# Soft-MoE behind banded attention: the last projection rounds dealt differently between output steps, one step split in two, three weight loads split in two

## The chip, the cores and the metric

One core of one Trainium2 chip runs the whole program. The metric is the time of one execution on the device in microseconds, and the median of three runs counts. Engines are named as in the profile: PE (TensorE, matmuls), DVE (VectorE), ACT (ScalarE), POOL (GpSimd) and SP (SyncE, which only issues transfers). SPq or PEq means the sequencer of an engine.

## The reference

Attention over 4 batches, 8 heads, 768 tokens and 64 features of a head, with a band of 96 keys, 8 global keys and a distance bias, is followed by a soft mixture of experts. Its tail is what this case is about:

```python
slot_input = d.T @ x                       # 32 slots, 4 for each of 8 experts
for e in range(E):
    h = np.maximum(slot_input[e] @ w1[e], 0.0)      # [4, 1024]
    slot_out[e] = h @ w2[e]                          # [4, 512]
c = softmax(logits, over the slots)        # [3072 tokens, 32 slots]
return c @ slot_out                        # [3072, 512], 6.29 MB in float32
```

## The kernel before

The first 140 us are attention and the softmax statistics, written as a long list of steps in a fixed order (`ORDER`); nothing there is touched. The tail follows in straight code at the end of `tile_attention_moe`, and the order in which it is written is the order on each engine: a manual schedule, in which every engine runs its instructions one after the other.

**Weights.** The two weight matrices of the experts lie in 32 pieces of 128 x 2048 float32 (1 MB). 24 of them have places of their own; the last eight (numbers 24 to 31, the second half of `w2` of experts 0 to 7) are loaded into places that the hidden layer has read. `load_w` issues them on SP, each as a first half (columns 0 to 1023) and a second half (1024 to 2047). Those second halves are the last loads of the program. The SP queue allows eight transfers under way: each issue waits for the landing of the one eight places before it.

**Projection.** The 512 output features are made in three parts, `OUT_PART`: 256, 128 and 128 wide. For a part, `project` multiplies the hidden values of all experts by `w2` in 16 rounds (eight blocks of the hidden dimension, for experts 0 to 3 and then 4 to 7); a round is four matmuls, one for each expert, each done in two passes in float32, and all rounds of a part add into one PSUM bank (line 154). `project_rounds(n, first, past)` issues some of the 16. Part 2 reads the second halves of pieces 24 to 31: rounds 0 to 7 those of pieces 24 to 27, rounds 8 to 15 those of 28 to 31.

**Slots.** When a part's rounds are done, `slots_raw` copies the bank to SBUF (ACT, line 183), `slots_spread` multiplies it by a spreading matrix (PE, line 192) and copies the result to the tile `sos` (DVE or ACT, line 193).

**Combine.** `combine(n, step)` makes output: four PSUM banks, one for each batch, and for each of the step's token tiles one matmul per batch (line 206); then ACT and DVE copy two banks each into halves of a staging buffer (line 211), and SP issues one transfer for batches 0 and 1 and one for 2 and 3 (line 212). `STEPS` says which token tiles a step has. The banks come from a ring of six (`LeftBanks`), so a step reuses banks of earlier steps and waits until those are copied. The staging halves are used in turn: `tb`, `v`, `tt`, `ph`, `xtt`, `xta`, `ph`, and again from `tb`.

**Order.** Rounds of part 1 stand between the steps of part 0, and rounds of part 2 around the steps of part 1, so that PE has work while a step's copies and transfers run. The steps of part 2 come last, one behind the other.

**The end.** Each engine then reads a flag and branches over a general path, which these inputs do not need (line 989). Behind it SP waits for its eight transfer semaphores, in the order of their numbers, and the engines meet at a barrier (line 1189).

Of the kernel before, what the change touches and what calls it, by code (L numbers as in the profile page):

```python
# [42 lines left out]
NS = E * SPE  # L43
HF = DM // 2
OUT_PART = ((0, 256), (256, 128), (384, 128))
STEPS = (tuple((0, 256, t, k) for t, k in ((0, 1), (1, 1), (2, 2), (4, 2))), tuple((0, 128, t, 3) for t in (0, 3)), tuple((0, 128, t, 2) for t in (0, 2, 4)))
BLOCKS = [(n, *step) for n in range(len(OUT_PART)) for step in STEPS[n]]
BLOCK_AT = [sum(4 * w * k for _, _, w, _, k in BLOCKS[:i]) for i in range(len(BLOCKS) + 1)]
XH = NJ * HF
# [19 lines left out]
class Moe:  # L69
# [125 lines left out]
    def combine(self, ps, ct, n, so, obs, out, step):  # L195


        nc = self.nc
        f, w, t0, k = STEPS[n][step]
        at = BLOCK_AT[sum(map(len, STEPS[:n])) + step]  # L200
        cps = [ps.tile([P, 512], F32, name="cp", tag="x") for _ in range(B)]
# [97 lines left out]
def tile_attention_moe(ctx: ExitStack, tc: tile.TileContext, qk, v, phi, w1, w2, nn, out):  # L299
# [29 lines left out]
    WP = 2048  # L329
# [46 lines left out]
    npl = len(places)  # L376
# [11 lines left out]
    def piece(k):  # L388
        m, r = divmod(k, 16)
        if m == 0:  # L390
            a, r = divmod(r, 8)
            half, s = divmod(r, 4)
        else:
            half, r = divmod(r, 8)
            a, s = divmod(r, 4)
        return m, 4 * a + s, half
# [3 lines left out]
    def load_w(pieces, c0=0, c1=WP):  # L400

        for k in pieces:
            m, e, half = piece(k)
            nc.sync.dma_start(out=places[k][:, c0:c1], in_=(w1, w2)[m][e][:, WP * half + c0:WP * half + c1])
# [520 lines left out]

    moe.hidden(left, Moe.slot_view(sl), w1_of, hs, ht, (reuse_first, reuse_second))
    load_w([31], WP // 4, WP // 2)
    load_w(range(npl + 1, 32), WP // 2, WP)

    obs = [places[16 + i // 2][:, 1024 * (i % 2):1024 * (i % 2) + 1024] for i in range(2 * (npl - 16))]  # L930
    ops = [xx[:, 0]]
# [2 lines left out]
    def project(n, a, cs=range(8)):  # L934
        moe.project(ops[n], ht, lambda e, h: places[where[1, e, h]], n, a, cs)
# [4 lines left out]
    def slots_raw(n):  # L940
        moe.slots_raw(ops[n], ows[:, parts[n]])

    def slots_spread(n, *copies):
        moe.slots_spread(left, ows[:, parts[n]], sos[:, parts[n]], copies)

    def combine(n, *steps):
        for step in steps:
            moe.combine(left, ct, n, sos[:, parts[n]], obs, out, step)

    def project_rounds(n, first, past):  # L950
        for k in range(first, past):
            project(n, k // 8, (k % 8,))
# [10 lines left out]
    weights(range(4), nc.vector.tensor_copy)  # L963
    slots_spread(0, nc.scalar.copy, nc.scalar.copy)
    ops += [left.keep(ops[0])] * 2
    project_rounds(1, 0, 4)
    combine(0, 0)
    project_rounds(1, 4, 7)
    combine(0, 1)
    project_rounds(1, 7, 11)  # L970
    combine(0, 2)
    project_rounds(1, 11, 16)
    slots_raw(1)
    combine(0, 3)
    slots_spread(1, nc.vector.tensor_copy)
    project_rounds(2, 0, 4)
    combine(1, 0)
    project_rounds(2, 4, 16)
    slots_raw(2)
    combine(1, 1)  # L980
    slots_spread(2, nc.vector.tensor_copy)
    combine(2, 0, 1, 2)
    order.close()
# [9 lines left out]
def general(ctx, tc, moe, qk, v, phis, w1, w2, ngl, nlo, ident, out):  # L993
# [114 lines left out]
    with ExitStack() as g3:  # L1108
# [27 lines left out]
        for n, (at, w) in enumerate(OUT_PART):  # L1136
# [5 lines left out]
            moe.slots_spread(ps, ow[:, c], so[:, c], (nc.vector.tensor_copy, nc.scalar.copy))  # L1142
            for step in range(len(STEPS[n])):
                moe.combine(ps, ct, n, so[:, c], obs, out, step)
# [53 lines left out]
```

## Time and profile before

| | us |
|---|---|
| median of 3 runs (187.65 to 188.02) | 187.96 |
| the profiled execution | 187.57 |
| its span in the profile | 185.6 |
| PE busy, share of the span | 169.5, 91% |
| DVE busy | 143.0, 77% |
| ACT busy | 125.5, 68% |
| POOL busy | 91.6, 49% |

The span is what the engines' instructions cover; the rest of the execution's 187.57 us lies around it. The shares are means over stages with different limits: PE is busy in nine slices of ten almost to the end, POOL has almost nothing to do from 125 us on, and in the last slices DMA is busy at 0.7 to 0.9 of its 16 engines while ACT and DVE are mostly idle. What a change in the tail does is read from the tail.

### The profile page before, as it was taken

What the parts mean: (1) busy time and instruction counts of PE and PEld (TensorE: products, weight loads), DVE (VectorE), ACT (ScalarE), POOL (GpSimd) and SP (SyncE); (2) the same over time, 40 slices, a digit from 0 to 9 for tenths busy, and PEclk for the clock granted to TensorE, in tenths of its full rate; (3) what the DMA queues carried; (4) which work ended last, traced back from release to release, by engine and by line L of the source; (5) the groups of instructions that cost most, each with busy time, mean ns of one, the idle gap of its engine ahead of it and who ended that gap; (6) DMA issues with size and microseconds to landing.
All of it is one profiled execution on the core that took longest, in us unless ns stands there. A gap on an engine that the chain in (4) does not pass through costs nothing. (4 is left out here: it accounts for less than half of the span.)

```text
span 185.6 us, 6743 instructions
## 1 busy us (share of the span) xinstructions
PE 169.5 (91%) x2811; PEld 126.4 (68%) x2811; DVE 143.0 (77%) x382; ACT 125.5 (68%) x163; POOL 91.6 (49%) x121
## 2 busy tenths in 40 slices
PE   8899899999998999999999997989899999999720
PEld 2567689897887698888879896674443256678610
DVE  5999999999999999899999899984686203345430
ACT  3499989999987989999999999933302110344320
POOL 6826689769868679588788778620010000000000
PEclk9999999999999999999999999999999999999995
DMA  6999999998998966979966699999999999889791
GB/s 204 415 414 369 405 403 385 360 368 248 379 342 319 361 203 169 390 272 333 371 221 201 222 289 412 401 346 408 353 354 331 419 401 411 350 308 400 300 351 45
DMA packets 15306, 61.41 MB, mean 331 GB/s; under 512 B 1698, under 2 KB 2850, under 8 KB 13474
## 3 DMA queue, kind: packets, MB, share of 16 engines
q1 hardware_dynamic: 15264, 60.89, 87.9%
q8 instruction: 24, 0.39, 0.8%
q14 instruction: 16, 0.13, 0.2%
q10 hardware_dynamic: 2, 0.00, 0.0%
HBM read 54.59 MB, written 6.29 MB: 328 GB/s over the span
## 5 line engine op out<-in xcount | busy, mean ns | idle before, releaser
L592 POOL TENSOR_TENSOR ph<-tb,ph 128x432 f16<-128x432 f32 x78 | 82.3, 1084 | 28.4 <-ACT ph L585 26.6
L582 ACT ACTIVATE tb<-tb,nb 128x1296 f32<-128x1296 f32 x32 | 43.5, 1374 | 1.6 <-DVE nb L578 1.5
L609 PEld LDWEIGHTS <-ph 128*128 128x128 f16 x1248 | 41.4, 97 | 3.8 <-issue 3.2
L609 PE MATMUL x<-v,ph 128*128 128x65 f16 (+1 forms) x1248 | 43.1, 193 | 0.4
L585 ACT CAST ph<-tb 128x1296 f16<-128x1296 f32 x32 | 40.7, 1271 | 3.1 <-PE x L609 1.9
L557 PE MATMUL sc<-raw 64*128 64x216 f32 (+1 forms) x392 | 39.3, 338 | 1.3 <-DVE mx L566 1.3
L557 PEld LDWEIGHTS sc<-raw 64*128 64x128 f32 x392 | 32.3, 186 | 6.1 <-DVE mx L566 2.7
L634 DVE CUSTOM_DVE_ANT_1 xn<-x,rc 120x448 f32<-120x448 f32 x32 | 18.8, 621 | 0.6
L566 DVE CUSTOM_DVE_ANT_1 tb<-sc,tt,mx 128x864 f32<-128x864 f32 x16 | 17.8, 1114 | 1.0 <-POOL ph L592 0.4
L646 PE MATMUL m<-ident,xn 120*128 120x120 f32 x105 | 16.1, 277 | 2.1 <-DVE nb L578 1.0
L535 DVE SCALAR_TENSOR_TENSOR v<-vt,v 128x896 f16<-128x896 f32 x14 | 15.2, 1085 | 0.2
L646 PEld LDWEIGHTS m<-ident,xn 120*128 120x128 f32 x105 | 10.7, 140 | 5.6 <-DVE nb L578 1.4
L592 DVE TENSOR_TENSOR ph<-tb,ph 128x432 f16<-128x432 f32 x18 | 13.4, 761 | 0.0
L101 PE MATMUL hp<-wp,sl 128*32 128x512 f32 x80 | 10.7, 593 | 0.0
L206 PE MATMUL cp<-sos,ct 32*128 32x128 f32 (+1 forms) x116 | 8.2, 332 | 1.3 <-DVE sos L193 1.1
L566 DVE CUSTOM_DVE_ANT_1 tb<-sc,xtt,mx 128x864 f32<-128x864 f32 x8 | 8.9, 1112 | 0.5 <-PE sc L557 0.4
L566 DVE CUSTOM_DVE_ANT_1 tb<-sc,xta,mx 128x864 f32<-128x864 f32 x8 | 8.8, 1101 | 0.1
L528 ACT ACTIVATE v<-vt 128x896 f16<-128x896 f32 x9 | 8.6, 953 | 0.0
L566 DVE CUSTOM_DVE_ANT_1 tb<-sc,tt 128x864 f32<-128x864 f32 x8 | 8.4, 1052 | 0.0
L154 PE MATMUL o<-wp,ht 128*32 128x128 f32 x256 | 8.2, 275 | 0.0
L154 PEld LDWEIGHTS o<-wp,ht 128*32 128x32 f32 x256 | 6.6, 110 | 1.4 <-issue 1.0
L101 PEld LDWEIGHTS hp<-wp,sl 128*32 128x32 f32 x80 | 2.9, 110 | 6.6 <-issue 6.3
(220 smaller groups left out, 277.7 us busy)
## 6 DMA issues: line engine op xcount, KB each, us to landing
raw<-in_qk_dram SPq DMA_DIRECT2D x14, 832.0 KB, 5.9
wp<-in_w_dram SPq DMA_DIRECT2D x10, 1024.0 KB, 8.1
wp<-in_w_dram SPq DMA_DIRECT2D x15, 512.0 KB, 9.0
vt<-in_v_dram SPq DMA_DIRECT2D x14, 448.0 KB, 5.1
tb<-in_w_dram SPq DMA_DIRECT2D x3, 1024.0 KB, 7.1
wp<-in_qk_dram SPq DMA_DIRECT2D x2, 832.0 KB, 9.2
raw<-in_w_dram SPq DMA_DIRECT2D x2, 832.0 KB, 5.8
ph<-in_w_dram SPq DMA_DIRECT2D x2, 768.0 KB, 8.3
```

The source lines that it names most:

```text
L101: self.nc.tensor.matmul(out=hp[n][32 * s:32 * s + 32, :], lhsT=slv(a, c, s), rhs=w1(4 * a + s, c // 2)[:, (c % 2) * DF + 512 * n:(c % 2) * ...
L154: nc.tensor.matmul(out=o[32 * s:32 * s + 32, o0:o0 + w], lhsT=ht[:, k:k + 32], rhs=w2(4 * a + s, half)[:, at:at + w], start=(a == 0 and c ...
L528: nc.scalar.activation(out=vhi[u % 2][:, :, :, 0:D], in_=vraws(u), func=AF.Copy, scale=V_SC)
L535: nc.vector.scalar_tensor_tensor(out=vlo[k].rearrange("p j i d -> p (j i) d"), in0=vraws(u).rearrange("p j i d -> p (j i) d"), scalar=V_SC ...
L557: nc.tensor.matmul(out=z[:, i, at:at + n], lhsT=r_[r, KCOL[j]:KCOL[j] + KR], rhs=r_[r, KW + KB * j:KW + KB * j + n], start=True, stop=True)
L566: nc.vector.tensor_tensor_reduce(out=tb(u)[:, :, BW * k:BW * k + BW], in0=sc[(3 * u + k) % 2][:, :, 0:BW], in1=table.unit(u % NP, k), scal ...
L582: nc.scalar.activation(out=t, in_=t, func=AF.Exp, bias=nbs[u], scale=T_SC)
L585: nc.scalar.copy(out=blocks(phi_[i])[:, :, 0:QW], in_=tb(u)[:, i].rearrange("p (s c) -> p s c", c=QW))
L592: (engine or nc.gpsimd).tensor_tensor(out=blocks(plo_[i])[:, c, 0:QW], in0=tb(u)[:, i].rearrange("p (s c) -> p s c", c=QW)[:, c], in1=bloc ...
L609: nc.tensor.matmul(out=x[:, (D + 1) * t:(D + 1) * t + d], lhsT=w[:, c:c + P], rhs=vv[:, j, i, 0:d], start=(z == 0), stop=(z == len(ops) - ...
L634: nc.vector.tensor_tensor_reduce(out=xnb[(u // 2) % 3][:, :, c:c + D], in0=xv[:, i, :, 0:D], in1=rcs.pop((u, i)).unsqueeze(2).to_broadcast ...
L646: nc.tensor.transpose(out=m[:, at:at + KB], in_=xnb[(u // 2) % 3][:, t, P * (p % 2):P * (p % 2) + P], identity=ident[0:KB, 0:KB])
```

## The change

It has three parts, all in the tail. The step of part 0 that makes token tiles 4 and 5 becomes two steps of one tile. The rounds are dealt anew: part 1 goes 2, 2, 2, 5, 5 rounds with a step of part 0 behind each (before 4, 3, 4, 5), and part 2 goes 4, 5, 7 with a step of part 1 behind the first two and the slot output behind the last (before 4, 12, with the second step of part 1 between the last round and the spread). And the second halves of pieces 29 to 31 are loaded in two transfers each: first the quarters for rounds 8 to 11, then those for rounds 12 to 15. The output blocks lie otherwise in DRAM (`BLOCK_AT`), and the host puts them in place as before.

```diff
-STEPS = (tuple((0, 256, t, k) for t, k in ((0, 1), (1, 1), (2, 2), (4, 2))), ...
+STEPS = (tuple((0, 256, t, k) for t, k in ((0, 1), (1, 1), (2, 2), (4, 1), (5, 1))), ...
...
     load_w([31], WP // 4, WP // 2)
-    load_w(range(npl + 1, 32), WP // 2, WP)
+    load_w(range(npl + 1, 29), WP // 2, WP)
+    load_w(range(29, 32), WP // 2, 3 * WP // 4)
+    load_w(range(29, 32), 3 * WP // 4, WP)
...
-    project_rounds(1, 0, 4)
+    project_rounds(1, 0, 2)
     combine(0, 0)
-    project_rounds(1, 4, 7)
+    project_rounds(1, 2, 4)
     combine(0, 1)
-    project_rounds(1, 7, 11)
+    project_rounds(1, 4, 6)
     combine(0, 2)
+    project_rounds(1, 6, 11)
+    combine(0, 3)
     project_rounds(1, 11, 16)
     slots_raw(1)
-    combine(0, 3)
+    combine(0, 4)
     slots_spread(1, nc.vector.tensor_copy)
     project_rounds(2, 0, 4)
     combine(1, 0)
-    project_rounds(2, 4, 16)
+    project_rounds(2, 4, 9)
+    combine(1, 1)
+    project_rounds(2, 9, 16)
     slots_raw(2)
-    combine(1, 1)
     slots_spread(2, nc.vector.tensor_copy)
     combine(2, 0, 1, 2)
```

PE, from the last round of part 2 to the first step of part 2, before (`o` is the bank of the projection, `wp_87` to `wp_91` the places of pieces 28 to 31, `x` and `cp` the banks of a step, `sp` that of the spread; the waits name an engine's or a transfer's semaphore, and the 49 behind it means nothing here):

```order
L154 MATMUL o<-wp_91,ht 32x128
L206 MATMUL cp<-sos,ct 128x128 [waits PE_49]
L206 MATMUL cp<-sos,ct 128x128
L206 MATMUL cp<-sos,ct 128x128 [waits Activation_49]
L206 MATMUL x<-sos,ct 128x128 [waits DVE_49]
L206 MATMUL cp<-sos,ct 128x128 x3
...
L192 MATMUL sp<-ows,spread 128x128 [waits Activation_49]
L206 MATMUL cp<-sos,ct 128x128 [waits DVE_49]
```

The same stretch in the changed kernel, from the end of the ninth round on:

```order
L206 MATMUL cp<-sos,ct 128x128 x2
L206 MATMUL cp<-sos,ct 128x128 [waits Activation_49]
L206 MATMUL cp<-sos,ct 128x128 [waits DVE_49]
L206 MATMUL cp<-sos,ct 128x128 x8
L154 MATMUL o<-wp_87,ht 32x128
...
L154 MATMUL o<-wp_88,ht 32x128 [waits DMAHW1_49]
L154 MATMUL o<-wp_90,ht 32x128 [waits DMAHW2_49]
L154 MATMUL o<-wp_91,ht 32x128 [waits DMAHW3_49]
...
L192 MATMUL sp<-ows,spread 128x128 [waits Activation_49]
L206 MATMUL x<-sos,ct 128x128 [waits DVE_49]
```

The second step of part 1 stands between two groups of rounds, three matmuls of the thirteenth round wait for loads of their own, and between the last round and the spread there is nothing more.

SP, the last loads and the first outputs, as the difference of the two (- before, + changed):

```order
 L404 DMA wp_87<-in_w_dram 128x1024
-L404 DMA wp_88<-in_w_dram 128x1024
-L404 DMA wp_90<-in_w_dram 128x1024
-L404 DMA wp_91<-in_w_dram 128x1024
+L404 DMA wp_88<-in_w_dram 128x512
+L404 DMA wp_90<-in_w_dram 128x512
+L404 DMA wp_91<-in_w_dram 128x512
+L404 DMA wp_88<-in_w_dram 128x512
+L404 DMA wp_90<-in_w_dram 128x512
+L404 DMA wp_91<-in_w_dram 128x512
 L212 DMA out_dram<-tb_95 128x512 x2
```

Three loads of 128 x 1024 become six of 128 x 512, ahead of the same first outputs.

SP's last output issues and its last waits before (`DMAHW0` to `DMAHW7` are the eight transfer semaphores; a transfer waits for, and then uses, the one named first):

```order
L212 DMA out_dram<-tb_95 128x512 [waits DMAHW0_49,DVE_49,Activation_49]
L212 DMA out_dram<-v_100 128x512 [waits DMAHW1_49,DVE_49,Activation_49]
L212 DMA out_dram<-v_100 128x512 [waits DMAHW2_49,DVE_49,Activation_49]
L989 COMPARE_AND_BRANCH
...
L989 UNCONDITIONAL_BRANCH
L989 UNCONDITIONAL_BRANCH [waits DMAHW0_49,DMAHW1_49,DMAHW2_49,DMAHW3_49,DMAHW4_49,DMAHW5_49,DMAHW6_49,DMAHW7_49]
```

And in the changed kernel:

```order
L212 DMA out_dram<-v_100 128x512 [waits DMAHW5_49,DVE_49,Activation_49]
L212 DMA out_dram<-tt 128x512 [waits DMAHW6_49,DVE_49,Activation_49]
L212 DMA out_dram<-tt 128x512 [waits DMAHW7_49,DVE_49,Activation_49]
L994 COMPARE_AND_BRANCH
...
L994 UNCONDITIONAL_BRANCH
L994 UNCONDITIONAL_BRANCH [waits DMAHW0_49,DMAHW1_49,DMAHW2_49,DMAHW3_49,DMAHW4_49,DMAHW5_49,DMAHW6_49,DMAHW7_49]
```

With five transfers more, the last one moves from semaphore 2 to semaphore 7, and the closing waits go through them from 0 to 7 in both.

## Rows read from the trace of the kernel before

**Rows 1.** Stages: window, its length, granted PE clock, DMA share, GB/s.

```profile
161.00:163.00 2.00, 1.00 0.65 254
163.00:165.00 2.00, 1.00 1.02 373
165.00:166.50 1.50, 1.00 0.50 190
166.50:173.50 7.00, 1.00 1.00 395
173.50:174.50 1.00, 1.00 0.14 52
...
181.00:183.50 2.50, 0.54 0.21 70
```

**Rows 2.** PE's timeline: start us, us, line, operation, count, idle before it.

```profile
159.42 1.08 PE L154 MATMUL o<-wp,ht 128*32 128x128 f32 x32
160.43 0.48 PE L206 MATMUL x<-sos,ct 32*128 32x256 f32 x1
...
161.07 0.86 PE L154 MATMUL o<-wp,ht 128*32 128x128 f32 x24
...
163.52 1.15 PE L206 MATMUL cp<-sos,ct 32*128 32x256 f32 x16
164.59 1.30 PE L154 MATMUL o<-wp,ht 128*32 128x128 f32 x40
165.82 0.48 PE L206 MATMUL x<-sos,ct 32*128 32x256 f32 x1
...
168.57 0.37 PE L206 MATMUL cp<-sos,ct 32*128 32x128 f32 x1 [0.17 <-DVE sos L193]
...
172.21 0.39 PE L206 MATMUL cp<-sos,ct 32*128 32x128 f32 x3
...
173.09 0.49 PE L192 MATMUL sp<-ows,spread 128*128 128x128 f32 x2
```

**Rows 3.** The chain that ended last: start us, us, what.

```profile
173.69 0.55 DVE xta L211
174.24 0.21 DVE sos L193
...
174.49 0.76 PE cp L206 x16
```

**Rows 4.** Timelines of DVE and ACT, columns as in rows 2.

```profile
161.20 0.76 DVE L211 COPY tb<-cp 128x256 f32<-128x256 f32 x2 [1.65 <-PE cp L206]
...
174.16 0.28 DVE L193 COPY sos<-sp 128x128 f32<-128x128 f32 x1
...
172.35 0.27 ACT L183 COPY ows<-o 128x128 f32<-128x128 f32 x1 [1.95 <-PE o L154]
```

**Rows 5.** SP's timeline, its last output issues.

```profile
176.83 1.41 SPq L212 DMA_DIRECT2D out_dram<-tb  x2
178.34 0.88 SPq L212 DMA_DIRECT2D out_dram<-v  x2
```

**Rows 6.** Line 989 in 177 to 186: operation, count, ns, first and last start.

```profile
L989 SPq EVENT_SEMAPHORE  x8: 17/17/17, 182.9 to 183.9; - x8
...
L989 ACTq COMPARE_BRANCH  x1: 50/50/50, 178.1 to 178.1; - x1
...
L989 SPq COMPARE_BRANCH  x1: 50/50/50, 179.3 to 179.3; - x1
L989 ACTq EVENT_SEMAPHORE  x1: 17/17/17, 182.1 to 182.1; - x1
```

**Rows 7.** Waits of SP's queue from 177.5: us in total, times, longest.

```profile
SPq L989 <- SPq L989: 4.1, 2, 3.6
```

**Rows 8.** Line 212 from 178.8: the last output transfer, issue to landing.

```profile
DMA to landing us min/median/max: 4.7/4.7/4.7
```

**Rows 9.** Line 404 in 137 to 155: the weight loads' issues and landings.

```profile
L404 SPq DMA_DIRECT2D wp<-in_w_dram x17: 327/378/1442, 137.4 to 154.1; - x17
...
DMA to landing us min/median/max: 7.5/9.1/10.6
```

More of the change, by code (lines that the diff above doesn't have):

```diff
@@ L45 @@
 OUT_PART = ((0, 256), (256, 128), (384, 128))
-STEPS = (tuple((0, 256, t, k) for t, k in ((0, 1), (1, 1), (2, 2), (4, 2))), tuple((0, 128, t, 3) for t in (0, 3)), tuple((0, 128, t, 2) for t in (0, 2, 4)))
+STEPS = (tuple((0, 256, t, k) for t, k in ((0, 1), (1, 1), (2, 2), (4, 1), (5, 1))), tuple((0, 128, t, 3) for t in (0, 3)), tuple((0, 128, t, 2) for t in (0, 2, 4)))
 BLOCKS = [(n, *step) for n in range(len(OUT_PART)) for step in STEPS[n]]
```

## The prediction, written before the changed kernel was run

> **What bounds the kernel now.** I read the page's slices first, then the stage table, the chain that ended last, the timelines of PE, ACT, DVE and SP in the last 27 us, and the waits of SP's queue. Up to 154 us the two programs issue the same work in the same order, so only the tail counts. In it three things run beside each other.
>
> DMA: the weight loads end near 161 us and the output transfers follow. The reader is to see that DMA is not the bound of the whole tail: its share falls to 0.65 in 161 to 163 and to 0.14 in 173.5 to 174.5, with 0.50 in 165 to 166.5 between full stretches [rows 1]. A stream with pauses is waiting for the engine that makes its data.
>
> PE makes it: from 159.42 it alternates projection rounds (L154, eight matmuls a round) with combine steps (L206), nearly without a wait [rows 2]. The last three combine steps can start only when the last part's slot output is spread: chain L183 (ACT), L192 (PE), L193 (DVE). In the chain of waits DVE reaches that copy at 174.24, right behind a copy of the step before, and PE starts at 174.49 [rows 3]. Call this start S. Behind S everything follows at fixed distance: copies, issues, and SP's last issue at about 178.84 (the last pair starts at 178.34 and takes 0.88) [rows 5].
>
> The end: SP branches at 179.3 and its first of eight waits at L989 ends at 182.9, the last at 183.9 [rows 6]. SP waited twice there, 3.6 us and then 4.1 - 3.6 = 0.5 us [rows 7]. The last transfer takes 4.7 us to land [rows 8], 178.84 + 4.7 = 183.5, which is the second wait. The first one is not a landing alone: ACT waits only for its own finished copies after its branch at 178.1, and yet its next instruction is at 182.1 [rows 6]. So an engine needs some 4 us to go on behind this branch, and SP pays 3.6 of it.
>
> [...]
>
> **The three split loads.** Three loads of 512 KB become six of 256 KB. Before, the last load is issued at 154.1 and lands after at most 10.6 us, by 164.7 [rows 9]. The rounds that read these pieces follow the step at 168.57 [rows 2], four rounds and more behind it, and after the change near 170.5, so PE does not wait now and will not wait then: gain 0, cover 5 us. The three more issues cost SP 3 x 0.38 = 1.1 us [rows 9], between 154 and the first output, when SP only waits. Each issue also waits for the transfer eight places ahead of it; with three transfers more that is three landings of 512 KB later, 3 x 0.524 MB / 0.395 = 4 us, about 158, still ahead of the queue's end at 161. Cost 0; if the cover went, 1.1 us would be added to the first output, which is not on the path that sets the end.
>
> [...] Streams of 256 KB outputs moved 373 GB/s (163 to 165), the mixed stretch of larger ones 395 [rows 1]: on 1.57 MB of loads and 1.05 MB of outputs made smaller this is 2.62/0.373 - 2.62/0.395 = 0.4 us of DMA time, ahead of the pause before S. [...] With up to eight transfers under way the row shows 6%, and the pause takes it.
>
> **The rounds dealt anew.** Costs from starts in the PE timeline [rows 2]: 4 rounds 160.43 - 159.42 = 1.01, 5 rounds 165.82 - 164.59 = 1.23, so 0.22 a round and 0.13 for each change to rounds. A combine step of one 256-wide tile 161.07 - 160.43 = 0.64, of two 164.59 - 163.52 = 1.07: 0.21 for each change to a step. A step of part 1 173.09 - 172.21 = 0.88.
> Before there are six stretches of rounds, after it eight: +0.27. The two-tile step split in two: +0.21. The second step of part 1 (0.88) moves from behind the last round to between the ninth and the tenth round of part 2: +0.88 on the last round. The wait of 0.17 ahead of the first step of part 1 goes, because the copies in front of DVE's slot copy are now those of a one-tile step, 0.76 for two [rows 4], half as wide as before: -0.17 [rows 2]. The last round of part 2 ends at 172.21 + 0.88 + 0.27 + 0.21 - 0.17 = 173.40 instead of 172.21.
> Then the spread: ACT copies 0.14 after the last round for 0.27 (172.35 against 172.21) [rows 2, 4], PE's spread follows 0.05 later and takes 0.49 [rows 2], DVE's copy, now with no other copy in front, 0.04 later for 0.28 [rows 4], 0.05 to PE: 173.40 + 0.14 + 0.27 + 0.05 + 0.49 + 0.04 + 0.28 + 0.05 = 174.72. So S is 0.23 LATER, although DVE's queue in front of it has gone: what was waited for in DVE is now spent on PE. What is late next is the plain chain from the last round to S, with PE idle.
>
> The earlier steps come earlier by up to 0.45 us (two rounds less ahead of the first), so DMA's pauses at 161 and 165 shrink; but the pause in front of S grows from 1 us to nearly 2, because the last output before it is issued about 1.3 us earlier. Filling early pauses is worth nothing by itself: nothing before S is still queued when the last transfers are issued.
>
> **The end, term by term.** (1) S +0.23, and the last issue and SP's branch with it. (2) SP waits for eight semaphores in number order. Before, the last transfer is on the third of them, so the five waits behind it (0.07 each: 1.0 us for all, less the 0.5 waited, over seven steps [rows 6, 7]) come after the landing. After, with five more transfers, it is on the eighth: seven waits pass while it lands. If it lands within 0.5 us of SP going on, the 0.5 us is gone: 0 to -0.5, taken -0.43, the 0.5 less one step. That needs a landing by 182.9 + 0.23 + 0.43 = 183.6, 4.5 us after an issue at 179.07; it took 4.7 before [rows 8], with some of the 16 DMA engines busy well behind the others (share 0.21 in 181 to 183.5 [rows 1]); the longer pause lets these catch up, and I count on it. (3) In SP's last six issues one pair takes 1.41 us for its two issues, the next 0.88 [rows 5]: a hold of 0.55 that pushes everything behind it. No wait of the program explains it. If it falls elsewhere or goes, -0.55; if it stays, 0. One pair of nine shows it, which speaks for its going; that all behind S keeps its distances speaks for its staying. I take half, -0.25.
> Sum +0.23 - 0.43 - 0.25 = -0.45 us. Bounds: +0.23 with terms 2 and 3 at nothing, -0.8 with both whole. The profiled execution took 187.57 (185.6 of span and 1.97 around it), 0.39 under the median of 187.96; on the median this is 187.5, between 187.2 and 188.2.
>
> **Rivals.**
> *No change that shows* (0.37). The hold stays, the last transfer straggles as before: +0.23 - 0.2 to -0.4, 187.75 to 188.0. For it: the chain behind S is the same work at the same distance. Against: the stragglers have a longer pause. If landings ruled as before and nothing else changed it would be 188.2.
> *All of it comes* (0.14). [...]
> *Slower: PSUM banks* (0.12). Steps now follow each other after two rounds. Six banks serve steps of four, so the second step needs two banks of the first: DVE starts its first copy 161.20 - 160.43 = 0.77 after the step's start and takes 0.38 of 0.76 for it [rows 2, 4]. The first step starts at 159.42 + 0.57 = 159.99 and gives its banks at 161.15; the second wants them at 161.21. With 0.06 to spare, a copy that begins 0.2 later at each of the four steps stalls PE by 0.6 to 0.8 in sum and S with it: -0.45 + 0.25 + 0.8 = +0.6, 188.6. It decides from 0.6 of stalls on. Against: copies start at steady distances in the trace.
> That the change does not do what it says is excluded for the rounds by their written order; for the loads it is the forecast itself (no effect).
>
> **How the numbers follow.** The forecast (a small gain, 187.2 to 187.7) has 0.37, its own value 187.5. 0.2%, 0.38 us, is about what a measurement of this kernel can tell from no change; that bound is 187.58, and of the forecast's 0.37 I count 0.32 as faster and 0.05 as same. With the rivals: faster 0.32 + 0.14 = 0.46, same 0.05 + 0.37 = 0.42, slower 0.12. The range 186.8 to 188.2 leaves out the slower rival and the extremes.
>
> **What would show it.** In the profile after: combine steps at about 159.99, 161.21, 162.43 and 164.73, last round ending near 173.4, the spread's DVE copy unqueued, and the last steps at 174.7; a DMA pause of nearly 2 us before 176.8 and smaller ones at 161 and 165; no wait of L154 on a load; SP's first L989 wait ending near 183.2 and its last within 0.6 of it. I am wrong if S moves ahead of 174.5, if PE waits for banks, or if the gain comes from the loads.

## The result, and the profile after

The changed kernel takes 188.95 us (median of 15 runs, 188.31 to 190.43) against 187.89 for the kernel before on the same chip (15 runs, 187.20 to 188.63): a ratio of 1.0066, 95% interval 1.0045 to 1.0086. It is slower by 0.7%, where 187.5 was forecast. Its profiled execution took 189.19 us with a span of 187.3 (before 187.57 and 185.6).

PE and DVE did what the prediction had worked out. PE's timeline after, for [rows 2] (start us, us, line, operation, count, idle before it):

```profile
160.03 0.48 PE L206 MATMUL x<-sos,ct 32*128 32x256 f32 x1
...
161.25 0.48 PE L206 MATMUL cp<-sos,ct 32*128 32x256 f32 x2
...
162.48 1.15 PE L206 MATMUL cp<-sos,ct 32*128 32x256 f32 x16
...
164.79 0.48 PE L206 MATMUL x<-sos,ct 32*128 32x256 f32 x1
...
171.73 1.74 PE L154 MATMUL o<-wp,ht 128*32 128x128 f32 x56
173.85 0.49 PE L192 MATMUL sp<-ows,spread 128*128 128x128 f32 x2 [0.38 <-ACT ows L183]
174.72 0.37 PE L206 MATMUL x<-sos,ct 32*128 32x128 f32 x1 [0.38 <-DVE sos L193]
```

The combine steps start at 160.03, 161.25, 162.48 and 164.79 (worked out: 159.99, 161.21, 162.43, 164.73). The last group of rounds ends at 173.47 (worked out from starts: 173.40; the ends in these rows are modelled), and S, the first matmul of the last part's steps, is at 174.72 (174.72). Up to S, PE has no idle time in these rows but the spread's and S's own.

DVE's copy of the slots, for [rows 4], is alone in its queue now:

```profile
174.37 0.29 DVE L193 COPY sos<-sp 128x128 f32<-128x128 f32 x1 [1.50 <-PE sp L192]
```

SP's last six issues, for [rows 5]:

```profile
175.99 1.06 SPq L212 DMA_DIRECT2D out_dram<-tb  x2
177.16 0.90 SPq L212 DMA_DIRECT2D out_dram<-v  x2
178.16 0.98 SPq L212 DMA_DIRECT2D out_dram<-tt  x2
```

The hold of 0.55 us that lay in the middle pair of the last six is gone from there; the first pair has one of 0.25 (1.06, where the undisturbed first pair of run 7 below takes 0.81). The last issue starts at 178.65, ahead of the 178.84 of before.

DMA by stage, for [rows 1] (window, length, five engines' busy time, granted PE clock, DMA share, GB/s), and the last output transfer, for [rows 8]:

```profile
161.00:163.00 2.00, 2.00 (x44) 1.26 (x40) 1.32 (x4) 1.06 (x4) 0.00 (x0) 1.00 0.75 283
165.00:166.50 1.50, 1.50 (x48) 1.13 (x44) 0.75 (x2) 0.65 (x2) 0.00 (x0) 1.00 0.89 351
173.50:174.50 1.00, 0.49 (x2) 0.30 (x2) 0.13 (x1) 0.27 (x1) 0.00 (x0) 1.00 1.00 399
176.00:177.00 1.00, 0.81 (x17) 0.62 (x17) 0.70 (x3) 0.54 (x3) 0.00 (x0) 1.00 0.23 80
```

```profile
DMA to landing us min/median/max: 4.9/4.9/4.9
```

The early pauses shrank (0.65 and 0.50 before), and the one in front of S moved behind it, to 176, where it is some 1 us and not the nearly 2 of the forecast. The last transfer takes 4.9 us to land, a little longer than the 4.7 of before; the prediction had counted on 4.5.

Line 994 in the changed kernel, for line 989 in [rows 6] (operation, count, ns, first and last start), and the wait row, for [rows 7] (us in total, times, longest):

```profile
L994 SPq EVENT_SEMAPHORE  x8: 17/17/17, 183.2 to 183.7; - x8
...
L994 ACTq COMPARE_BRANCH  x1: 50/50/50, 178.8 to 178.8; - x1
...
L994 SPq COMPARE_BRANCH  x1: 45/45/45, 179.2 to 179.2; - x1
...
L994 ACTq EVENT_SEMAPHORE  x1: 17/17/17, 182.9 to 182.9; - x1
```

```profile
SPq L994 <- SPq L994: 3.9, 1, 3.9
```

SP goes on at 183.15 (forecast 183.2) and its last wait is at 183.71, 0.2 ahead of before, within 0.6 of the first as forecast. There is one stall instead of two. Up to this point the changed kernel leads by 0.2 us.

It loses 1.9 us behind it. SP then has eight more waits of the closing code, two DRAINs, and a barrier with the other engines, all at one line of the source, 1189 before and 1194 after. Before, from SP's last wait there to just behind the second DRAIN:

```profile
L1189 SPq DRAIN  x2: 7/7/7, 184.5 to 184.5; - x2
L1189 SPq EVENT_SEMAPHORE  x1: 28/28/28, 184.4 to 184.4; - x1
```

And after, from the first DRAIN on:

```profile
L1194 SPq DRAIN  x2: 7/67/127, 184.3 to 186.1; - x2
```

```profile
L1194 POOLq EVENT_SEMAPHORE  x1: 17/17/17, 186.2 to 186.2; - x1
```

The reader is to see the two starts of DRAIN: 184.46 and 184.52 before, 184.32 and 186.06 after. Between these two neighbouring instructions SP stands still for 1.75 us, where it took 0.06, and no engine runs an instruction in that time that could have held it or let it go. POOL, which opens the barrier, goes on at 186.2 (before 184.55), and everybody leaves it at 187.2 (185.5). The wait view has no row for this gap, since no semaphore ends it.

### The profile page after: what moved, and what is told of

Same layout as the page of the kernel before. It is cut to its first block, busy times and chain, and to the rows that moved or that the text cites. A ratio compares the mean times of both kernels' runs of the same rounds, so it can differ in the third digit from the quotient of the medians.

```text
span 187.3 us, 6759 instructions
## 1 busy us (share of the span) xinstructions
PE 170.7 (91%) x2811; PEld 126.5 (68%) x2811; DVE 143.1 (76%) x384; ACT 125.6 (67%) x165; POOL 91.7 (49%) x121
## 4 chain that ended last, share of the span: by engine, by line
```

## The experiments

**The theory.** SP's code got longer. The program before has 436 SP instructions ahead of the target of its last branch, the changed one 447 (five transfers with two waits on the path that runs, and two with two waits in the fallback that it jumps over, which uses the same `STEPS`). The author's guess, tested by the runs below and called the code-page theory in what was expected of them: if an engine's code is brought to it in pieces, the pages, then the closing stretch of 21 instructions, 8 waits and 13 more, may now lie across the border of two of them, and SP stands still until the second is there. The trace has packets on a queue of kind "instruction" (queue: packets, MB, share), in 180.4 to 181.4 and in 183.0 to 184.5 of the changed kernel:

```profile
q14 instruction: 3, 0.02, 6.6%
```

```profile
q14 instruction: 3, 0.02, 5.4%
```

That is two rounds of three packets of 8 KB (0.14 MB in the 17 of the whole execution), the last packets of each starting at 181.21 and 183.83; SP moves on 1.94 us behind the one, at 183.15, and 2.23 behind the other, at 186.06. Which engine a packet serves is not recorded, so this is a hint and no proof; that the stall is a fetch of code stays an inference in all that follows, while the place of the code is what the runs vary. **The rivals:** the stall comes from the new rounds and steps, or from the split loads, by whatever they leave in the queues.

Dead transfers, put into the fallback, move the closing stretch and change nothing that runs (K of them; the builder adds one wait, and four where K is 120):

```diff
     nc.gpsimd.memset(sl, 0.0)
+    gpad = gk.tile([P, K], F32, name="gpad")
+    for i in range(K):
+        nc.sync.dma_start(out=gpad[:, i:i + 1], in_=w2[0][:, i:i + 1])
     with ExitStack() as g0:
```

**1. The changed kernel, K = 30.**

> The changed kernel with 30 more transfers in the fallback branch, which is not run: on SP they and one wait stand between the last executed branch and its target, so SP's closing stretch stands 31 instructions further on in its code and nothing that runs is altered. Code-page theory: after it SP's closing stretch no longer straddles the border at which the changed kernel's SP stood still for 1.75 us between its two DRAINs; that gap shrinks to the 0.06 of the kernel before, the span falls by 1.69 to about 185.6, the time to 187.2 to 187.5, ratio to before 0.996 to 1.000. Rival, the stall belongs to the new rounds, steps or loads (a landing, a queue): nothing that runs has changed, so the gap of 1.75 and the ratio of 1.0066 stay.

Measured: 187.36 us (12 runs), ratio 0.9993 (0.9976 to 1.0010); the span is 185.4. The two DRAINs (same columns as above):

```profile
L1197 SPq DRAIN  x2: 7/7/7, 184.3 to 184.3; - x2
```

The gap is gone and with it the loss, although rounds, steps and loads are those of the changed kernel. The instruction queue has its three packets in 183 to 184.5 here too (two in the kernel before, which has no gap either): a packet there does not hold SP by itself, and what differs is the place of the code.

**2. The kernel before, K = 10**, which puts its closing stretch where the changed kernel has it.

> The kernel before with 10 more transfers in the fallback branch that is not run (11 SP instructions with a wait), so that SP's closing stretch stands just where it stands in the changed kernel, while tail and loads are those of before. Code-page theory: a gap of 1.3 to 1.8 us appears between SP's two DRAINs, the span grows from 185.6 to 187.0 to 187.4, ratio 1.006 to 1.010. Rival, the stall belongs to the rounds, steps or loads: no gap, ratio 1.000 within 0.002.

Measured: 188.99 us (7 runs), ratio 1.0080 (1.0051 to 1.0109), span 186.8 (a little under what was expected):

```profile
L1192 SPq DRAIN  x2: 7/67/127, 184.3 to 185.7; - x2
```

A gap of 1.33 us between the same two DRAINs, with the old tail. Code that never runs made the old kernel as slow as the new one.

**3. The changed kernel, K = 12**, border among the closing waits.

> The changed kernel with 12 more dead transfers (13 SP instructions): by the code-page theory the border now falls among SP's eight waits for the output's landings (behind about the fifth) and not between its DRAINs. If the next page's arrival at about 186.1 sets the time at which the stretch goes on, everything behind the border still has to be run after it: eight waits and the DRAIN, 0.6 to 1.0 us more, so the end comes at 188.0 to 188.3, time 189.6 to 190, ratio 1.010 to 1.014, slower still than the changed kernel. First rival, the fetch is hidden while SP waits for the outputs anyway: no gap, ratio 0.996 to 1.000. Second rival, the stall has nothing to do with the place of the code: ratio 1.0066 as the changed kernel, gap between the DRAINs.

Measured: 189.41 us (6 runs), ratio 1.0094 (1.0066 to 1.0122), span 187.7. SP's waits at line 994 up to 183.6, and from there on:

```profile
L994 SPq EVENT_SEMAPHORE  x4: 17/17/17, 183.1 to 183.4; - x4
```

```profile
L994 SPq EVENT_SEMAPHORE  x4: 17/17/17, 185.7 to 186.0; - x4
```

Four waits, a gap from 183.41 to 185.70, four waits. The gap moved by exactly the 13 instructions of the shift (17 instructions ahead of the border, now 4). It was expected behind the fifth; in that count a branch stood that isn't executed. The gap was not hidden beside the output transfers: the first rival of this run is out. SP went on at 185.7 and not 186.06, so the span is 0.4 us longer than the changed kernel's and not 0.6 to 1.0, and the ratio is just under the range given; the two kernels' intervals overlap.

**4. The kernel before, K = 30.**

> Control: the kernel before with 30 dead transfers (31 SP instructions), so that its closing stretch stands wholly behind the border. Code-page theory: no gap, span 185.4 to 185.8, ratio 1.000 within 0.002. Rival, more code in the branch that is not run costs by its amount (a longer jump): ratio above that of the kernel with 10, over 1.006.

Measured: 187.56 us (12 runs), ratio 0.9988 (0.9969 to 1.0008); no gap. Its profiled execution was one of the longer ones (188.18, span 186.3; its first output is issued 0.57 us late already, at 162.26 against 161.69, and one issue at 179.52 holds SP for 1.47), so the span missed the range while the runs met it. Part of that is PE's pace, and not the dead code: its first six matmuls of line 546 take 2.68 us where they took 1.47, and near the end its granted clock is 0.62 in 177 to 178 and 0.50 from 178 on, where the kernel before has 1.00 up to 181; in 175 to 180 PE is busy for 3.12 us and not 2.10. The mean granted clock of this execution is 0.976, as in the profiled one of run 6 (188.15 us), where the kernel before has 0.988. More dead code costs nothing by its amount.

**5. Rounds and steps alone, loads as before.**

```diff
-    load_w(range(npl + 1, 29), WP // 2, WP)
-    load_w(range(29, 32), WP // 2, 3 * WP // 4)
-    load_w(range(29, 32), 3 * WP // 4, WP)
+    load_w(range(npl + 1, 32), WP // 2, WP)
```

> The new rounds and the split step alone, the three loads whole as before: SP's closing stretch of 21 instructions then begins 8 instructions further on than in the kernel before and 3 less far than in the changed kernel. The border that the first four runs put 17 instructions behind the first closing wait of the changed kernel then falls before the very last instruction, SP's last barrier event. Code-page theory: the gap moves there; SP's last event waits until about 186.0 where it would run at 185.3, so 0.6 to 0.8 us are lost and not 1.7, span 186.0 to 186.3, ratio 1.003 to 1.005. Rival A, the loss comes from the rounds and steps: ratio 1.0066, gap between the DRAINs. Rival B, from the split loads: ratio 1.000.

Measured: 187.55 us (12 runs), ratio 0.9997 (0.9978 to 1.0015). The barrier's last events:

```profile
L1192 POOLq EVENT_SEMAPHORE  x1: 17/17/17, 185.4 to 185.4; - x1
...
L1192 PEldq EVENT_SEMAPHORE  x1: 51/51/51, 185.4 to 185.4; - x1
L1192 SPq EVENT_SEMAPHORE  x1: 17/17/17, 186.2 to 186.2; - x1
```

The gap is where it was expected, ahead of the last instruction: the other engines leave at 185.4, SP at 186.17, and the span is 186.2. But the time did not follow. What lies around the span shrank to 187.57 - 186.2 = 1.4 us, from the 1.97 of before, and 10 of the 12 runs have 1.3 to 1.5: the time after the span seems to begin when the other engines are done, not at SP's last event. The place was predicted, the price was not.

**6. The split loads alone** (the diff of the change for `load_w`, nothing else).

> The three split loads alone, rounds and steps as before: SP's closing stretch begins 3 instructions further on than before and ends ahead of the border. Code-page theory: no gap, the split loads cost nothing, ratio 1.000 within 0.002. Rival, the split loads bring the loss (more issues, later landings): ratio 1.006, PE waiting for a load in 163 to 172.

Measured: 187.83 us (12 runs), ratio 1.0006 (0.9993 to 1.0018); no gap (DRAINs at 184.81 and 184.87), and no wait of PE for a load in 155 to 178. Neither half of the change loses anything; only both together push the DRAIN over the border.

**7. The changed kernel with a short jump.** The fallback's loads go out on ACT's queue, so that SP's branch skips 41 instructions and not 262.

```diff
-                    nc.sync.dma_start(out=qt, in_=qk[b, h // 2, r0:r0 + D, KW:])
+                    nc.scalar.dma_start(out=qt, in_=qk[b, h // 2, r0:r0 + D, KW:])
...                                      (so for kt, vt and the weights)
```

> The changed kernel with the fallback branch's 128 loads issued from ACT's queue and not from SP's; that branch is not run. [...] Code-page theory with fetching ahead of the next page: SP goes on right behind its branch at about 179.2 and not 4 us later, its eight waits end with the last landing (183.2 to 183.5), no gap later; the end comes 0.1 to 0.4 earlier than with 30 dead transfers, span 185.0 to 185.3, ratio to before 0.996 to 0.999. Rival, every taken branch costs a fetch wherever it goes: first closing wait at 183.1 as before, span 185.4, ratio 0.999 to 1.000.

Measured: 186.76 us (12 runs), ratio 0.9950 (0.9925 to 0.9976), span 184.8, a little faster than the 0.996 to 0.999 expected. Line 994 on SP, and its waits in all (columns as for the changed kernel):

```profile
L994 SPq EVENT_SEMAPHORE  x8: 17/17/17, 179.7 to 183.1; - x8
...
L994 SPq COMPARE_BRANCH  x1: 50/50/50, 179.2 to 179.2; - x1
```

```profile
SPq L994 <- SPq L994: 3.6, 4, 2.2
```

SP goes on 0.5 us behind its branch and not 4. Six waits pass by 180.42, the seventh at 182.59, and the last one passes at 183.15, 0.02 behind the landing of the last transfer (183.13). In 183 to 184.5 the instruction queue has two packets where the changed kernel has three:

```profile
q14 instruction: 2, 0.02, 3.3%
```

This version beats both kernels.

**8. The kernel before with the same short jump.**

> The kernel before with the same edit of the branch that is not run. What the new rounds, step and loads are worth with no code fetch at SP's end is the difference between this and the changed kernel with the same edit. My tail theory (0.2 us late on TensorE, some tenths won in SP's issue and waits) says 0 to 0.3 us slower than that one, ratio to before 0.998 to 1.000; rival, the tail change is worth nothing: the same time.

Measured: 187.57 us (12 runs), ratio 0.9999 (0.9983 to 1.0014), span 185.2:

```profile
L989 SPq EVENT_SEMAPHORE  x8: 17/17/17, 182.0 to 183.5; - x8
...
L989 SPq COMPARE_BRANCH  x1: 50/50/50, 179.4 to 179.4; - x1
```

```profile
173.78 0.81 SPq L212 DMA_DIRECT2D out_dram<-xta  x2
175.71 1.31 SPq L212 DMA_DIRECT2D out_dram<-ph  x2
177.13 0.88 SPq L212 DMA_DIRECT2D out_dram<-tb  x2
178.11 1.27 SPq L212 DMA_DIRECT2D out_dram<-v  x2
```

The last transfer lands at 183.16, nearly as in run 7. But the third wait is the one that waits for it, and five more follow, until 183.53. With the code in place the new tail is worth 0.4 us in the two profiled executions (186.78 and 187.17) and 0.8 in the medians, more than the 0.3 expected; the intervals against the kernel before don't meet.

Part of those 0.8 goes with PE's clock and not with the tail. Six of this run's twelve executions have a mean granted clock of 0.974 to 0.977 and take 187.74 us in the median, six have 0.982 to 0.989 and take 187.23; all twelve of run 7 have 0.982 to 0.991. Compared at the upper clock, run 7 is ahead by 0.5. The kernel before, on the same chip, takes 188.00 in its 13 executions of 0.974 to 0.979 and 187.56 in the 21 of 0.980 to 0.989. So at like clocks this run is ahead of the kernel before by about 0.3, and its waits end 0.36 earlier; the ratio of 0.9999 hides that. Why an execution has the one clock or the other, and why none of run 7's has the lower one, was not tested.

**9. Run 7 with 120 dead transfers back on SP.**

> [...] Code-page theory: the fetch of about 4 us behind the branch is back, first closing wait at 183.1, no gap later, span 185.4, time 187.2 to 187.4, ratio to before 0.997 to 1.000. Rival, the seventh run won by having the fallback's loads off SP's queue and not by the distance: first closing wait right behind the branch at 179.7, span 184.8, ratio 0.995.

Measured: 187.35 us (12 runs), ratio 0.9979 (0.9958 to 1.0000), span 185.3:

```profile
L994 SPq EVENT_SEMAPHORE  x8: 17/17/17, 183.1 to 183.6; - x8
...
L994 SPq COMPARE_BRANCH  x1: 45/45/45, 179.1 to 179.1; - x1
```

The 4 us behind the branch are back, with the loads still off SP's queue: it is the distance of the jump that counts (165 instructions, and 41 in run 7).

## Why the prediction was wrong, point by point

**What failed** is the end of the sum: it stops at SP's last closing wait and takes what follows for fixed, 185.6 - 183.9 = 1.7 us as before [rows 6]. After, it was 187.26 - 183.71 = 3.55. The prediction knew the stall behind the branch, read it off ACT's and SP's rows (4.0 and 3.6 us) and counted the added transfers for the order of the waits; it did not ask whether the instructions added on SP move the code behind the branch over a border. The missing term is +1.75 - 0.06 = 1.7 us. Runs 1 to 3 show that it comes and goes with the place of SP's closing code alone; that code is being fetched meanwhile is the author's reading, with the packets as a hint. This term alone turns a lead of 0.2 into the loss: 185.6 - 0.2 + 1.7 is 187.1, and 187.3 was measured (the second DRAIN itself took 0.12 longer).

**Term 1**, S +0.23, is right to 0.01, and the parts in front of it to 0.02 (the spread at 173.85 for 173.86, DVE's copy at 174.37 for 174.39). The copies in front of DVE's slot copy are gone, and PE's added work took their place.

**Term 2**, the order of the waits, -0.43, is right as it was counted: from SP's first wait to its last it is 0.94 us before and 0.54 after, -0.41. The lead at the last wait is only 0.2, because SP goes on 0.2 later than before (183.15 for 182.95). The prediction had that too, but by the branch, which was to move with S under a stall of fixed length. In fact the branch comes 0.09 earlier, and SP goes on 3.96 us behind it and not 3.67 (3.05 in run 4): the right 183.2 was in part luck. DVE, which branches 0.63 later than before, goes on just ahead of SP in both (182.81 and 183.08); whether one engine's stall depends on another's was not tested. The last landing was at 183.50 and in the first run at 183.20, when SP was running its waits one by one from 183.15 on; so what ends last is the stall behind the branch, plus eight waits of 0.07 to 0.09. Where that stall is taken away, the order pays as much: 183.15 in run 7 against 183.53 in run 8, -0.38.

**Term 3**, the hold in SP's issues, was guessed at half of 0.55 for want of a cause. Eleven profiles say more. Time above 0.45 us an issue, over the last six issues: 0.48, 0.35, 1.58, 0.67 and 0.69 us with the old rounds, 0.22 once and 0.08 or 0.09 five times with the new ones. So the hold went, by about 0.6 on average, and the last issue came earlier although S was later (178.63 in run 7, 178.82 in run 8). In the changed kernel it brings nothing at the end: it is what brings the branch forward, and the longer stall behind the branch takes it back. In the new order issues of 0.6 to 1.4 us stand at 166 to 171, where nothing waits for them. Why an issue takes so long was not tested.

**The split loads** cost 0, as forecast (run 6, ratio 1.0006). **The rivals:** PE waited for no bank ahead of S (from 155 to 174.7 its one wait is the spread's, 0.4 us). "No change that shows" is what rounds, steps and loads are worth as long as the stall behind the branch ends last (run 1, ratio 0.9993), for the reason given there in part: it named the last landing, and it was that stall. "All of it comes", terms 2 and 3 whole at the bound of -0.8, did not come in the changed kernel, and its 0.14 in the sum for faster was the author's estimate; run 7, 186.76 us, goes past it, with SP going on 0.5 us behind its branch and not 4, but it takes an edit of code that does not run.

**The length of the jump.** SP goes on 3.96 us behind a jump over 262 instructions (the changed kernel), 3.99 behind one over 165 (run 9), and 0.51 behind one over 41 (run 7). Where between 41 and 165 the stall begins, how far one border lies from the next, and whether the next page is fetched ahead of its use, as the expectation of run 7 assumed, no run shows: these were the author's guess. Behind a far branch SP stood still a second time for 0.8, 1.33, 1.75 and 2.29 us (run 5, run 2, the changed kernel, run 3) and not at all in runs 1 and 4. In the straight code ahead of the branch no gap of this kind was looked for.

## What to carry to other kernels

Where a program ends behind a far branch (here one over 262 instructions), count the instructions between the target and the end on the engine that closes it: whether a border like this one lies among them is worth 0.7 to 0.9% here, and an added transfer, even in code that never runs, can put it there. So before a small loss or gain is put down to a schedule, look for an idle stretch that no semaphore ends, and move the code by some dead instructions to see whether it stays. Better still, keep the jump short: together with the new tail it saved 0.5% here (run 7); with the old tail the ratio shows nothing (run 8). And before two medians are compared, look whether their executions had the same clock.

## What the runs showed of the hardware

SP goes on 4.0 us behind the far branch of the changed kernel and of run 9, and 0.5 behind the near one of run 7. In the changed kernel and in runs 2, 3 and 5 it stops a second time, at one fixed place of the code: what lies behind that border ran 2.55 (run 3) to 2.94 us (run 5) after SP had gone on, and the changed kernel, which reaches its first DRAIN in 1.2 us, comes to the border first. Dead code has no price by its amount (run 4) and a price of 1.3 us by its place (run 2). A stall of 0.8 us on the last instruction of SP cost nothing that shows (run 5: ratio 0.9997, run 1 without it 0.9993).
